# Two of the output's 32 weight heads, loaded in 64 small pieces between the K and V loads

## The chip, the core and the metric

The kernel runs on one core of a Trainium2 chip. Its time is the device time of one execution in microseconds (us). PE is TensorE (matmuls, with their weight loads shown as PEld), ACT is ScalarE, DVE is VectorE, POOL is GpSimd, SP is SyncE, from whose queue nearly all transfers are issued; 16 transfer (DMA) engines carry them out.

## The reference

One step of decoding: attention with a long cache, multiplied by a gate that a small dense block computes. All is float32.

```python
# x: 2 x 1 x 512; 32 query heads, 8 K/V heads, 32768 cached keys, 128 per head; wq 512 x 4096, wo 4096 x 512
xn = layernorm(x)
q = (xn @ wq) as 2 x 32 x 1 x 128
scores = q . k_cache * 128 ** -0.5        # each K/V head serves 4 query heads
o = softmax(scores) . v_cache             # 2 x 32 x 128
s = o as 2 x 4096 @ wo                    # the output's weights: 32 heads of 128 x 512
h = max(xn @ w1 + b1, 0) ** 2             # 512 -> 1792
g = silu(h @ w2 + b2)                     # 1792 -> 512
return x + s * g
```

K and V are 2 x 8 x 32768 x 128 numbers each, 268 MB, and are read once.

## The kernel before

The host lays the inputs out so that each transfer is a plain block. The 16 pairs of a batch entry and a K/V head (`NS`) are the turns of a loop. Each turn takes four blocks of 128 rows by 64 KB, 8192 KB each: K in two halves (transposed, `in_kt`), V in two halves (`in_vt`). They go in turn into two tiles in SBUF, `slot0` and `slot1`; the query weights (`in_wq`) and the dense block's weights (`in_wm`) are the first two blocks that pass through these slots.

PE, ACT and DVE run the turns in a hardware loop; SP and POOL have their instructions written out. In a turn, `scores(0)` and `scores(1)` multiply K's halves with the queries into the PSUM banks `sc`; DVE and PE find the maximum, ACT takes the exponentials, PE transposes them (`tp`, `pT`), and two passes over V's halves add up in `o_ps`; at the end of the turn these are copied, transposed (`ot`) and scaled into a column of `oT`. Behind each pass over a slot PE counts its semaphore up, and `release` issues the next load into that slot, which waits in SP's queue for this count. So while one load runs, the next one is issued as soon as PE is through with the other slot. An instruction in SP's queue that waits holds up those behind it.

The output's weights `wo` have a place of their own in SBUF, `wo_sb`, 32 heads of 512 numbers on each of 128 rows. They are issued from SP directly behind the last V load, in pieces of 16, 8, 5 and 2 heads (`PIECES`) and one more head in two halves, each with a semaphore of its own (`piece0` to `piece5`). After the loop PE multiplies heads 0 to 23 as they come (the matmuls into `wb`, in which each head is one matmul 512 wide), ACT copies their sum, and PE adds it up together with heads 24 to 31 in `sc` (matmuls 64 wide); DVE multiplies by the gate and adds x in one scan, and SP stores the result. The gate comes from the dense block, which runs before the loop.

`AHEAD` is a number of semaphore clears that SP runs between the load of `in_wm` and the first K load; they have no effect on the data.

Of the kernel before, what the change touches and what calls it, by code (L numbers as in the profile page):

```python
# [15 lines left out]
P = 128  # L16
B, D, HQ, HKV, SK, DH, F = 2, 512, 32, 8, 32768, 128, 1792
REP = HQ // HKV
NS = B * HKV
# [6 lines left out]
FJ = FG // 32  # L26
SLOT = HALF
NSLOT = 2
PIECES = (16, 8, 5, 2)
WIDE = 24  # L30
AHEAD = 9
HN = P // 2
SCALE = 1.0 / math.sqrt(DH)

# [88 lines left out]
        return self.sem, self.n  # L123


def build(nc, x22, x8, kt, vt, wq, wm, wo, out):
    pe, act, dve = (Looped(nc, e, n) for e, n in ((nc.tensor, "pe"), (nc.scalar, "act"), (nc.vector, "dve")))
    pool, sp = (Engine(nc, e, n) for e, n in ((nc.gpsimd, "pool"), (nc.sync, "sp")))

    def mm(*args, **kw):  # L130
        pe.do("matmul", *args, **kw)
# [4 lines left out]
    def sb(name, *shape):  # L136
        return nc.alloc_sbuf_tensor(name, [P, *shape], F32)

    slots = [sb(f"slot{i}", SLOT) for i in range(NSLOT)]
    wo_sb = sb("wo_sb", HQ * D)  # L140
# [15 lines left out]

    slot_sem = [nc.alloc_semaphore(f"slot{i}") for i in range(NSLOT)]
    piece_sem = [nc.alloc_semaphore(f"piece{i}") for i in range(len(PIECES) + 2)]
    small_sem, xe_sem, out_sem = (nc.alloc_semaphore(n) for n in ("small", "xe", "out"))
    count = [0] * NSLOT  # L160
    free = [None] * NSLOT
# [2 lines left out]
    def load(src, width):  # L164
        i = issued[0] % NSLOT
        issued[0] += 1
        if free[i] is not None:
            sp.wait(free[i])
        count[i] += 16
        nc.sync.dma_start(slots[i][:, 0:width], src).then_inc(slot_sem[i], 16)  # L170
        return i, (slot_sem[i], count[i])

    stream = [load(wq, SLOT), load(wm, 2 * FJ * D)]
    for _ in range(AHEAD):
        nc.sync.sem_clear(out_sem)
    todo = [(x[s, u], SLOT) for s in range(NS) for x in (kt, vt) for u in range(2)]

    def release(token):
        free[stream.pop(0)[0]] = token
        if todo:  # L180
            stream.append(load(*todo.pop(0)))
            if not todo:
                h = 0
                for n, sem in zip(PIECES, piece_sem):
                    nc.sync.dma_start(wo_sb[:, h * D:(h + n) * D], wo[h * P:(h + n) * P].rearrange("(p h) e -> p (h e)", h=n)).then_inc(sem, 16)
                    h += n
                for u in range(2):
                    nc.sync.dma_start(wo_sb[:, h * D + u * NG * HN:h * D + (u + 1) * NG * HN],
                                      wo[h * P + u * HN:h * P + (u + 1) * HN].rearrange("r (t e) -> (r t) e", t=2)).then_inc(piece_sem[len(PIECES) + u], 16)


    g = nc.gpsimd
    t = pool.done(g.memset(ident[:, :], 0.0))
# [12 lines left out]
    for u in range(2):  # L206
# [5 lines left out]
    t = dve.done("tensor_reduce", selh[:, :], ident[:, :].rearrange("p (a h) -> p h a", h=REP), axis=AX.X, op=ALU.add)  # L212
# [10 lines left out]
    t = pe.done()  # L223
    dve.wait(t)
    t = dve.done("tensor_copy", xs[:, :], ms[:, 0:22])
    pe.wait(t, t_one)
    mm(ms[:, 32:40], mean[:, :], xs[:, 0:8], start=True, stop=True)
    t = pe.done()
    dve.wait(t)
    t = dve.done("tensor_reduce", st[:, 2:4], ms[:, 32:40].rearrange("p (d b) -> p b d", b=B), axis=AX.X, op=ALU.add)  # L230
    dve.wait(t)
    t = dve.done("tensor_tensor", xc[:, :].rearrange("p (d b) -> p d b", b=B), xs[:, 0:8].rearrange("p (d b) -> p d b", b=B),
                                 st[:, None, 2:4].to_broadcast([P, ND, B]), op=ALU.add)
    dve.wait(t)
    t = dve.done("tensor_mul", sq[:, :], xc[:, :], xc[:, :])
    pe.wait(t)
    mm(ms[:, 64:72], mean[:, :], sq[:, :], start=True, stop=True)
    t = pe.done()
    dve.wait(t)
    t = dve.done("tensor_reduce", st[:, 4:6], ms[:, 64:72].rearrange("p (d b) -> p b d", b=B), axis=AX.X, op=ALU.add)  # L240
    dve.wait(t)
    t = dve.done("tensor_scalar", st[:, 6:8], st[:, 4:6], -1.0, 1e-5, op0=ALU.mult, op1=ALU.add)
    act.wait(t)
    t = act.done("activation", st[:, 8:10], st[:, 6:8], AF.Sqrt)
    dve.wait(t)
    t = dve.done("reciprocal", st[:, 10:12], st[:, 8:10])
# [5 lines left out]
    i, t = stream[0]  # L252
    pe.wait(t_x, t, t_selg)
    for d in range(ND):
        for f in range(2):
            for c in range(NG):
                lo = d * HQ * DH + (f * NG + c) * W
                mm(sc[f][32 * c:32 * c + 32, :], xT[:, d, :], slots[i][:, lo:lo + W], start=(d == 0), stop=(d == ND - 1))
    t = pe.done()
# [3 lines left out]
    for f in range(2):  # L263
# [3 lines left out]
        t = pe.done()  # L267
# [70 lines left out]
    for s in range(NS):  # L338
# [4 lines left out]
        t_s, t = scores(1)  # L343
# [3 lines left out]
        t = dve.done("tensor_reduce", r1[:, :], rm[:, :], axis=AX.X, op=ALU.max)  # L347
        pe.wait(t, *([t_rs] if t_rs else []))
        tr(ms[:, :P], r1[:, :].to_broadcast([P, P]), ident[:, :])
        t = pe.done()  # L350
        dve.wait(t)
        t = dve.done("tensor_reduce", mh[:, :], ms[:, :P].rearrange("p (a h) -> p h a", h=REP), axis=AX.X, op=ALU.max)
        dve.wait(t)
        t = dve.done("tensor_mul", mm4[:, :], mh[:, :], seln[:, :])
        dve.wait(t)
        t = dve.done("tensor_reduce", nm[:, :], mm4[:, :], axis=AX.X, op=ALU.add)
# [5 lines left out]
        for u in range(2):  # L362
# [3 lines left out]
            t = pe.done()  # L366
# [4 lines left out]
        t = pe.done()  # L371
        dve.wait(t)
        t_rs = dve.done("reciprocal", rs[:, :], ms[:, :REP])
        for u in range(2):
            i, t = stream[0]
            pe.wait(t, t_pT[u], t_osb)
            for n in range(32):
                y = n % NG
                k, r = divmod(n, 8)
                lo = k * 32 + r * 4  # L380
# [7 lines left out]
        for n in range(4):  # L388
            lo = n * (P - REP)
# [11 lines left out]
    def heads(h, u):  # L401
        hkv, k = divmod(h, REP)
        lo = 2 * hkv * REP * 16 + (1 - u) * REP + k
        return oT[:, lo:lo + 31 * REP + 1:REP]
# [3 lines left out]
    h = 0  # L408
# [6 lines left out]
        for c in range(NG):  # L415
            mm(acc[32 * c:32 * c + 32, 0:2 * HN:2], heads(h, u), wt[:, h, los[c]:los[c] + HN], start=False, stop=stop)

    for n, sem in zip(PIECES, piece_sem):
        if h == WIDE:
            pe.wait(t_w)  # L420
            for u in range(2):
                for c in range(NG):
                    lo = c * P + u * HN
                    mm(acc[32 * c:32 * c + 32, 0:2 * HN:2], selg[:, 32 - u:64 - u], o_sb[:, lo:lo + HN], start=(u == 0), stop=False)
        pe.wait((sem, 16))
        for h in range(h, h + n):
            if h < WIDE:
                c = h % NG
                mm(wb[32 * c:32 * c + 32, :], heads(h, 0), wt[:, h, :], start=(h < NG), stop=(h >= WIDE - NG))
                if h == WIDE - 1:  # L430
                    t = pe.done()
                    act.wait(t, t_otr)
                    t_w = act.done("copy", o_sb[:, :], wb[:, :])
                continue
            pe.wait(t_res)
            if h // REP == HKV - 1:
                pe.wait(t_o)
            for u in range(2):
                narrow(h, u, [c * P + u * HN for c in range(NG)], False)
        h += 1  # L440
    for u in range(2):
        pe.wait((piece_sem[len(PIECES) + u], 16))
        narrow(h, u, [(u * NG + c) * HN for c in range(NG)], u == 1)
    t = pe.done()
    dve.wait(t, t_gate)
    t = dve.done("tensor_tensor_scan", yb[:, :], gate[:, :], acc[:, :2 * HN], 0.0, op0=ALU.mult, op1=ALU.add)
    sp.wait(t)
    nc.sync.dma_start(out, yb[:, :]).then_inc(out_sem, 16)
    used = sorted(x.num for x in [e.sem for e in (pe, act, dve, pool, sp)] + slot_sem + piece_sem + [small_sem, xe_sem])
    nc.sync.sem_clear(range(used[0], used[-1] + 1))  # L450
    nc.sync.wait_ge(out_sem, 16)
    for e in (pe, act, dve):
# [8 lines left out]
def packed(A_x, A_k_cache, A_v_cache, A_wq, A_wo, B_w1, B_b1, B_w2, B_b2):  # L461

    def c(a):
        return np.ascontiguousarray(a)

    x = np.asarray(A_x).reshape(B, D)
    k = np.asarray(A_k_cache).transpose(1, 0, 3, 2).reshape(NS, DH, 2, HALF).transpose(0, 2, 1, 3)
    v = np.asarray(A_v_cache).transpose(1, 0, 2, 3).reshape(NS, 2, NG, NJ, 4, P, DH).transpose(0, 1, 5, 4, 2, 3, 6).reshape(NS, 2, P, SLOT)
    wq = np.asarray(A_wq).reshape(ND, P, HQ * DH).transpose(1, 0, 2).reshape(P, SLOT)
    w1 = np.asarray(B_w1).reshape(ND, P, F).transpose(1, 0, 2).reshape(P, ND * F)  # L470
    w2 = np.asarray(B_w2).reshape(NG, FJ, 32, D).transpose(0, 2, 1, 3).reshape(P, FJ * D)
    w = np.asarray(A_wo).reshape(HQ, DH, D)
    parts, h = [], 0
    for n in PIECES:
        parts.append(w[h:h + n].transpose(1, 0, 2).reshape(n * P, D))
        h += n
    last = w[h].reshape(DH, NG, 2, HN)
    parts += [last[:, :, u].reshape(HN, D) for u in range(2)]
    rows = [x.reshape(B, ND, P).transpose(1, 0, 2).reshape(B * ND, P),
            np.asarray(B_b1).reshape(NG, FJ, 32).transpose(1, 0, 2).reshape(FJ, P)]  # L480
    x4 = x.reshape(B, NG, 2, HN).transpose(2, 1, 0, 3)
    b4 = np.repeat(np.asarray(B_b2).reshape(NG, 2, HN).transpose(1, 0, 2)[:, :, None], B, axis=2)
    eight = [a.reshape(2 * NG * B, HN) for a in (x4, b4)]
    return {"x22": c(np.concatenate(rows)), "x8": c(np.concatenate(eight, axis=1)), "kt": c(k), "vt": c(v), "wq": c(wq),
            "wm": c(np.concatenate([w1, w2], axis=1)), "wo": c(np.concatenate(parts))}


# [13 lines left out]
```

## Time and profile before

| | us |
|---|---|
| median of 3 runs | 1302.91 (1302.81 to 1303.24) |
| the profiled execution | 1302.98 |
| its span, from first to last instruction | 1301.7 |
| busy: PE / PEld / ACT / DVE / POOL | 672.9 / 208.6 / 79.1 / 49.5 / 5.6 |
| K and V loads | 64 of 8192 KB |
| bytes read from HBM | 561.01 MB |
| mean granted clock of PE | 0.734 of full speed |

The profile gives for each engine its busy time, then transfers by queue, then the chain of work that ended last, followed back from the last instruction. Busy times are averages over stages with different limits, so the stages are also read one by one: as windows of time, as the chain in order of time, and as lists of waits, in which "A <- B" means that A stood idle until B was done. For a transfer the time from issue to landing includes the time for which it queued behind others. Nearly all instructions of PE, ACT and DVE carry one line number, that of the helper that puts them into the program (L64), so groups are named by their tiles.

### The profile page before, as it was taken

The numbers are of one execution on the slowest core, as the hardware profiler recorded it, in microseconds if no ns is written. First come the engines' busy times: TensorE is split into PE (matmuls) and PEld (weight loads), VectorE is DVE, ScalarE is ACT, GpSimd is POOL, SyncE is SP. The second block draws the span as 40 slices with busy tenths as digits, with TensorE's granted clock in tenths as the row PEclk, the third lists the DMA queues.
The fourth block names the chain that finished last, engine by engine and source line by source line (L and its number), as shares of the span: only waits on it lengthen the run. The fifth ranks groups of instructions, "written<-read, shape, count | busy, mean of one in ns | idle before, by whom it ended". The sixth has DMA issues, their size and how long they took to land.

```text
span 1301.7 us, 10377 instructions
## 1 busy us (share of the span) xinstructions
PE 672.9 (52%) x4713; PEld 208.6 (16%) x4713; DVE 49.5 (4%) x165; ACT 79.1 (6%) x139; POOL 5.6 (0%) x30
## 2 busy tenths in 40 slices
PE   3445445535536545545645545554654654554565
PEld 1111111211112111111211111121111211111122
DVE  0000000000000000000000000000000000000000
ACT  1010010100001010010101001010010101001010
POOL 0000000000000000000000000000000000000000
PEclk9777677678677778667677767767767767767777
DMA  9999999999999999999999999999999999999998
GB/s 412 428 446 425 443 425 445 419 443 427 429 441 427 443 427 443 423 445 421 443 427 427 443 427 443 427 443 421 445 423 441 429 427 443 427 443 425 445 421 363
DMA packets 10583, 561.17 MB, mean 431 GB/s; under 512 B 1195, under 2 KB 1617, under 8 KB 1745
## 3 DMA queue, kind: packets, MB, share of 16 engines
q1 hardware_dynamic: 10512, 561.06, 99.7%
q8 instruction: 5, 0.08, 0.0%
q10 hardware_dynamic: 65, 0.02, 0.0%
q14 instruction: 1, 0.01, 0.0%
HBM read 561.01 MB, written 0.07 MB: 431 GB/s over the span
## 4 chain that ended last, share of the span: by engine, by line
DMA 75%; PE 24%; issue 1%; DVE 0%; ACT 0%; SPq 0%; ACTq 0%
DMA slot<-in_vt 36%; DMA slot<-in_kt 36%; PE sc L64 12%; PE o_ps L64 11%; DMA slot<-in_wm 3%; PE wb L64 1%; DVE hT L64 0%; ACT o_sb L64 0%; DVE o_sb L64 0%; PE ot L64 0%; DVE yb L64 0%; SPq L170 0%; ACT sc L64 0%; ACTq L454 0%; ACTq L102 0%
## 5 line engine op out<-in xcount | busy, mean ns | idle before, releaser
L64 PE MATMUL sc<-slot,qz 128*32 128x512 f32 x2048 | 295.5, 742 | 299.6 <-DMA slot<-in_kt 299.6
L64 PE MATMUL o_ps<-slot,pT 128*16 128x512 f32 x2048 | 294.4, 739 | 209.0 <-DMA slot<-in_vt 209.0
L64 PEld LDWEIGHTS sc<-slot,qz 128*32 128x32 f32 x2048 | 81.0, 133 | 503.3 <-issue 503.3
L64 PEld LDWEIGHTS o_ps<-slot,pT 128*16 128x16 f32 x2048 | 69.3, 113 | 420.7 <-issue 420.7
L64 ACT ACT_TABLE_LOAD x19 | 24.4, 1283 | 650.3 <-DVE nm L64 647.3
L64 PE MATMUL tp<-ident,prob 128*128 128x128 f32 x136 | 31.2, 403 | 53.2 <-ACT prob L64 53.2
L64 DVE TENSOR_REDUCE rm<-sc 128x1 f32<-128x512 f32 x32 | 22.1, 691 | 574.9 <-PE sc L64 574.9
L64 ACT COPY o_sb<-o_ps 128x512 f32<-128x512 f32 x16 | 9.4, 586 | 504.8 <-PE o_ps L64 504.8
L64 PEld LDWEIGHTS tp<-ident,prob 128*128 128x128 f32 x136 | 24.0, 206 | 57.7 <-issue 55.7
L64 DVE TENSOR_REDUCE t<-ot 128x4 f32<-128x64 f32 x16 | 3.6, 224 | 524.2 <-PE ot L64 524.2
L64 ACT ACTIVATE prob<-sc,nm 128x512 f32<-128x512 f32 x32 | 21.7, 683 | 0.2
L64 ACT COPY pT<-tp 128x512 f32<-128x512 f32 x32 | 18.8, 586 | 13.8 <-PE tp L64 13.8
L64 PE MATMUL sc<-slot,xT 128*32 128x512 f32 x64 | 8.6, 695 | 17.7 <-DMA slot<-in_wq 17.7
L64 PE MATMUL ot<-ident,o_sb 128*128 128x128 f32 x64 | 10.1, 280 | 13.7 <-ACT o_sb L64 12.8
L64 PEld LDWEIGHTS ms<-selh,l 128*128 128x128 f32 x64 | 15.6, 334 | 0.0
L64 PE MATMUL ms<-ident,r 128*128 128x128 f32 x16 | 4.7, 294 | 20.0 <-DVE r L64 20.0
L64 PE MATMUL ms<-selh,l 128*128 128x4 f32 x64 | 13.7, 319 | 0.0
L64 PEld LDWEIGHTS ot<-ident,o_sb 128*128 128x128 f32 x64 | 6.7, 141 | 27.9 <-issue 27.9
L64 PE MATMUL wb<-slot,xT 128*32 128x448 f32 x32 | 4.8, 762 | 6.4 <-DMA slot<-in_wm 6.4
L275 POOL COPY qz<-qT 128x4 f32<-128x4 f32 x16 | 3.0, 187 | 1167.2 <-PE sc L64 1137.2
L64 PEld LDWEIGHTS ms<-ident,r 128*128 128x128 f32 x16 | 2.1, 133 | 34.1 <-issue 34.1
L64 ACT ACTIVATION_READ_ACCUMULATOR prob<-sc,nm 128x1 f32 x32 | 6.3, 196 | 0.0
(63 smaller groups left out, 55.4 us busy)
## 6 DMA issues: line engine op xcount, KB each, us to landing
slot<-in_wm SPq DMA_DIRECT2D x1, 7168.0 KB, 38.4
wo_sb<-in_wo SPq DMA_DIRECT2D x1, 4096.0 KB, 39.1
wo_sb<-in_wo SPq DMA_DIRECT2D x1, 2048.0 KB, 43.5
wo_sb<-in_wo SPq DMA_DIRECT2D x1, 1280.0 KB, 45.8
slot<-in_kt SPq DMA_DIRECT2D x32, 29.1
slot<-in_vt SPq DMA_DIRECT2D x32, 29.1
wo_sb<-in_wo SPq DMA_DIRECT2D x1, 512.0 KB, 46.6
wo_sb<-in_wo SPq DMA_DIRECT2D x2, 128.0 KB, 46.4
```

The costliest lines, as they stand in the source:

```text
L64: instruction = getattr(self.e, name)(*[x(i) if callable(x) else x for x in args], **kw)
L275: return pool.done(g.tensor_copy(qz[:, 28:32], qT[:, b, hkv, :]))
```

## The change

The first piece has 14 heads instead of 16. The two heads that it loses, 0 and 1 (`EARLY`), get an input of their own, `in_we`, cut by the host into 64 blocks of 16 rows of 512 bytes, 8 KB each. Behind each of the 64 K and V loads, `bit` issues one of these blocks from the same queue into its place in `wo_sb`: 32 for head 0 (8 groups of 16 rows, 4 quarters of the width), then 32 for head 1. Each head's 32 blocks count on one semaphore (`early0`, `early1`), and PE waits for each count ahead of that head's first matmul. `AHEAD` goes from nine to one. The last V load, the weights' remaining pieces and PE's matmuls stay in their order.

```diff
-PIECES = (16, 8, 5, 2)
+PIECES = (14, 8, 5, 2)
+EARLY = HQ - 1 - sum(PIECES)
 WIDE = 24
-AHEAD = 9
+AHEAD = 1
...
+    def bit():
+        n = 2 * NS * 2 - len(todo) - 1
+        h, n = divmod(n, 4 * P // 16)
+        g, q = divmod(n, 4)
+        lo = h * D + q * P
+        nc.sync.dma_start(wo_sb[16 * g:16 * g + 16, lo:lo + P], we[h, g, q]).then_inc(early_sem[h], 16)
+
     def release(token):
         free[stream.pop(0)[0]] = token
         if todo:
             stream.append(load(*todo.pop(0)))
+            bit()
             if not todo:
-                h = 0
+                h = EARLY
...
-    for n, sem in zip(PIECES, piece_sem):
+    parts = [(1, (sem, 16 * (4 * P // 16))) for sem in early_sem] + [(n, (sem, 16)) for n, sem in zip(PIECES, piece_sem)]
+    for n, t in parts:
...
-        pe.wait((sem, 16))
+        pe.wait(t)
...
+    early = w[:EARLY].reshape(EARLY, P // 16, 16, 4, P).transpose(0, 1, 3, 2, 4)
+    parts, h = [], EARLY
```

SP's queue at the start, from the loads of the query weights and of the dense block on. An entry gives its line, what it moves, and in brackets the semaphore for which it waits (`pe` is PE's count). Before:

```order
L170 DMA slot<-in_wq 128x16384 [waits barrier_Pool_Activation_PE_DVE_SP_release]
L170 DMA slot<-in_wm 128x14336
L175 ISA x9
L170 DMA slot<-in_kt 128x16384 [waits pe] x2
L170 DMA slot<-in_vt 128x16384 [waits pe] x2
L170 DMA slot<-in_kt 128x16384 [waits pe] x2
```

And now:

```order
L172 DMA slot<-in_wq 128x16384 [waits barrier_Pool_Activation_PE_DVE_SP_release]
L172 DMA slot<-in_wm 128x14336
L177 ISA
L172 DMA slot<-in_kt 128x16384 [waits pe]
L185 DMA wo_sb<-in_we 16x128
L172 DMA slot<-in_kt 128x16384 [waits pe]
L185 DMA wo_sb<-in_we 16x128
L172 DMA slot<-in_vt 128x16384 [waits pe]
```

A small load, which waits for nothing itself, stands between each load and the wait of the next; of the nine clears one is left.

SP's queue at the end, from the last two V loads on. Before:

```order
L170 DMA slot<-in_vt 128x16384 [waits pe] x2
L185 DMA wo_sb<-in_wo 128x8192
L185 DMA wo_sb<-in_wo 128x4096
L185 DMA wo_sb<-in_wo 128x2560
L185 DMA wo_sb<-in_wo 128x1024
L188 DMA wo_sb<-in_wo 128x256 x2
L448 DMA out<-yb 128x128 [waits dve]
```

And now:

```order
L172 DMA slot<-in_vt 128x16384 [waits pe]
L185 DMA wo_sb<-in_we 16x128
L172 DMA slot<-in_vt 128x16384 [waits pe]
L185 DMA wo_sb<-in_we 16x128
L195 DMA wo_sb<-in_wo 128x7168
L195 DMA wo_sb<-in_wo 128x4096
L195 DMA wo_sb<-in_wo 128x2560
L195 DMA wo_sb<-in_wo 128x1024
```

The last small load stands ahead of the first piece, which is two heads narrower (7168 numbers a row instead of 8192); the pieces behind it are the same.

PE behind the loop, where the heads' matmuls begin. Before:

```order
L64 MATMUL wb<-wo_sb,oT 32x512 [waits piece0]
L64 MATMUL wb<-wo_sb,oT 32x512 x15
L64 MATMUL wb<-wo_sb,oT 32x512 [waits piece1]
L64 MATMUL wb<-wo_sb,oT 32x512 x7
L64 MATMUL sc<-o_sb,selg 32x64 [waits act]
```

And now:

```order
L65 MATMUL wb<-wo_sb,oT 32x512 [waits early0]
L65 MATMUL wb<-wo_sb,oT 32x512 [waits early1]
L65 MATMUL wb<-wo_sb,oT 32x512 [waits piece0]
L65 MATMUL wb<-wo_sb,oT 32x512 x13
L65 MATMUL wb<-wo_sb,oT 32x512 [waits piece1]
L65 MATMUL wb<-wo_sb,oT 32x512 x7
```

The same 24 matmuls stand in the same order; the first two wait for the small loads' counts and no longer for the first piece.

More of the change, by code (lines that the diff above doesn't have):

```diff
@@ L123, in done, with build @@
         return self.sem, self.n
-def build(nc, x22, x8, kt, vt, wq, wm, wo, out):
+def build(nc, x22, x8, kt, vt, wq, wm, we, wo, out):
     pe, act, dve = (Looped(nc, e, n) for e, n in ((nc.tensor, "pe"), (nc.scalar, "act"), (nc.vector, "dve")))
@@ L158, in build @@
     piece_sem = [nc.alloc_semaphore(f"piece{i}") for i in range(len(PIECES) + 2)]
+    early_sem = [nc.alloc_semaphore(f"early{i}") for i in range(EARLY)]
     small_sem, xe_sem, out_sem = (nc.alloc_semaphore(n) for n in ("small", "xe", "out"))
@@ L181, in release @@
             stream.append(load(*todo.pop(0)))
+            bit()
             if not todo:
-                h = 0
+                h = EARLY
                 for n, sem in zip(PIECES, piece_sem):
-                    nc.sync.dma_start(wo_sb[:, h * D:(h + n) * D], wo[h * P:(h + n) * P].rearrange("(p h) e -> p (h e)", h=n)).then_inc(sem, 16)
+                    nc.sync.dma_start(wo_sb[:, h * D:(h + n) * D], wo[(h - EARLY) * P:(h - EARLY + n) * P].rearrange("(p h) e -> p (h e)", h=n)).then_inc(sem, 16)
                     h += n
@@ L188, in release @@
                     nc.sync.dma_start(wo_sb[:, h * D + u * NG * HN:h * D + (u + 1) * NG * HN],
-                                      wo[h * P + u * HN:h * P + (u + 1) * HN].rearrange("r (t e) -> (r t) e", t=2)).then_inc(piece_sem[len(PIECES) + u], 16)
+                                      wo[(h - EARLY) * P + u * HN:(h - EARLY) * P + (u + 1) * HN].rearrange("r (t e) -> (r t) e", t=2)).then_inc(piece_sem[len(PIECES) + u], 16)
     g = nc.gpsimd
@@ L448, in build @@
     nc.sync.dma_start(out, yb[:, :]).then_inc(out_sem, 16)
-    used = sorted(x.num for x in [e.sem for e in (pe, act, dve, pool, sp)] + slot_sem + piece_sem + [small_sem, xe_sem])
+    used = sorted(x.num for x in [e.sem for e in (pe, act, dve, pool, sp)] + slot_sem + piece_sem + [small_sem, xe_sem] + early_sem)
     nc.sync.sem_clear(range(used[0], used[-1] + 1))
@@ L472, in packed @@
     w = np.asarray(A_wo).reshape(HQ, DH, D)
-    parts, h = [], 0
+    early = w[:EARLY].reshape(EARLY, P // 16, 16, 4, P).transpose(0, 1, 3, 2, 4)
+    parts, h = [], EARLY
     for n in PIECES:
@@ L484, in packed @@
     return {"x22": c(np.concatenate(rows)), "x8": c(np.concatenate(eight, axis=1)), "kt": c(k), "vt": c(v), "wq": c(wq),
-            "wm": c(np.concatenate([w1, w2], axis=1)), "wo": c(np.concatenate(parts))}
+            "wm": c(np.concatenate([w1, w2], axis=1)), "we": c(early), "wo": c(np.concatenate(parts))}
 def kernel(**inputs):
```

## The prediction

> **What bounds the kernel now.** I read the page first: the busy shares, the transfers, the chain that ended last.
>
> ```profile
> PE 672.9 (52%) x4713; PEld 208.6 (16%) x4713; DVE 49.5 (4%) x165; ACT 79.1 (6%) x139; POOL 5.6 (0%) x30
> DMA  9999999999999999999999999999999999999998
> q1 hardware_dynamic: 10512, 561.06, 99.7%
> DMA 75%; PE 24%; issue 1%; DVE 0%; ACT 0%; SPq 0%; ACTq 0%
> ```
>
> No compute engine is busy for more than half of the span, while the packets of SyncE's queue (q1) fill 99.7% of 16 transfer engines. The chain gives PE 24% all the same, so the next view is the chain in order of time, to see whether PE's share is a real second bound. Columns: start, length, what.
>
> ```profile
> 50.24 29.31 DMA slot<-in_kt
> ...
> 1202.35 9.32 PE o_ps L64 x64
> ...
> 1240.95 8.81 PE sc L64 x64
> 1249.76 0.02 issue
> 1249.78 29.75 DMA slot<-in_vt
> 1279.53 0.22 issue
> 1279.75 9.88 PE o_ps L64 x64
> ...
> 1291.06 5.36 PE wb L64 x48
> 1296.42 0.02 issue
> 1296.45 0.59 ACT o_sb L64
> 1297.04 0.04 issue
> 1297.09 2.52 PE sc L64 x142
> 1299.60 0.02 issue
> 1299.62 0.42 DVE yb L64
> ```
>
> The chain goes from a landing to PE's 9 us on that slot, from there to the issue of the next load into it, and 29 us later that load lands. But only the first part of those 29 us is free: the load issued at 1249.78 stands behind the one issued before it, which is still running. The pace shows it. The load that landed at 50.24 + 29.31 = 79.55 is the second of the 64 K and V loads, the one at 1279.53 is the last, 62 loads further: (1279.53 - 79.55)/62 = 19.354 us for 8192 KB, 433 GB/s. The windows say that nothing is idle there (columns: window, its length, busy of each engine, granted clock, DMA share, GB/s):
>
> ```profile
> 98.86:1240.84 1141.98, 593.46 (x4018) 180.76 (x4018) 39.13 (x129) 63.43 (x113) 2.62 (x14) 0.72 1.00 433
> 1279.75:1285.38 5.63, 5.63 (x28) 1.28 (x32) 0.00 (x0) 0.00 (x0) 0.00 (x0) 0.50 0.99 425
> 1285.38:1289.62 4.24, 4.20 (x40) 0.94 (x32) 0.00 (x0) 0.00 (x0) 0.00 (x0) 1.00 0.95 406
> ```
>
> So up to the last V landing at 1279.53 the time is bytes over a full pipe: share 1.00 for 1142 us. From there PE leads: 9.88 us on V, the copy and transposes, 48 matmuls on `wb` in 5.36, the copy, `sc` in 2.52, the scan, the store. Beside it runs the transfer of the output's weights, 8192 KB (4096 + 2048 + 1280 + 512 + 2 x 128). Whether that ends before PE or after decides what a smaller remainder is worth, so the third reading is the issues and landings of these pieces (KB each, us from issue to landing; then SyncE's issues with their start):
>
> ```profile
> wo_sb<-in_wo SPq DMA_DIRECT2D x1, 4096.0 KB, 39.1
> wo_sb<-in_wo SPq DMA_DIRECT2D x1, 512.0 KB, 46.6
> wo_sb<-in_wo SPq DMA_DIRECT2D x2, 128.0 KB, 46.4
> out<-yb SPq DMA_DIRECT2D x1, 64.0 KB, 1.6
> ```
> ```profile
> 1250.15 2.12 SPq L185 DMA_DIRECT2D wo_sb<-in_wo  x4
> 1251.85 0.42 SPq L185 DMA_DIRECT2D wo_sb<-in_wo  x1
> 1252.32 0.91 SPq L188 DMA_DIRECT2D wo_sb<-in_wo  x2
> ```
>
> The first piece lands at 1250.15 + 39.1 = 1289.25, the 512 KB piece at 1251.85 + 46.6 = 1298.45, the last half at about 1252.80 + 46.4 = 1299.2 (the second issue of the pair starts some 0.48 behind the first). PE's `sc` group ends at 1297.09 + 2.52 = 1299.61, and its last four matmul pairs are the only ones that need that half. Transfers and PE end within a few tenths of each other. PE's waits in the last 22 us say the same:
>
> ```profile
> PE o_ps L64 <- DMA slot<-in_vt: 10.1, 1, 10.1
> PEld wb L64 <- DMA wo_sb<-in_wo: 0.4, 1, 0.4
> ```
>
> The one wait put down to the output's weights is 0.4 us of a weight load, and the matmuls of the group behind it run on without a break (48 in 5.36 us is 0.11 each). Taking bytes away here therefore frees at most about 0.4 us, and likelier nothing.
>
> **The change part by part.**
>
> *512 KB leave the first piece* (16 heads become 14). At 19.354/8192 = 2.363 ns per KB this is 1.21 us of transfer behind the last V landing. PE leads there, so I cost it at zero; bounds 0 to -0.4 us from the row above.
>
> *64 loads of 8 KB join the stream.* Their bytes are the same 1.21 us in sum, 0.0189 us each, but 63 of the 64 now run ahead of the last V landing, in a window whose DMA share is 1.00: no gap takes them up. On top comes what a transfer costs beyond its bytes, which no row shows for 8 KB. The nearest rows are the five pieces that queue behind the first: from 1289.25 to 1299.2, 9.95 us for 4096 KB, where bytes give 9.68, so 0.27 more or 0.055 a piece. Each has 128 rows, 8 for each of 16 engines if they are shared out evenly, and a completion. If the 0.055 is spread over these nine, a small load (16 rows, so one row and one completion for each engine) costs 0.012; if all of it is the completion, 0.055; at the low end nothing. I take 0.012, an even sharing, since no row sets a completion apart from the data rows beside it. So 0.031 us a load (0.019 to 0.074), and the last V lands 63 x 0.031 = 1.95 us later (1.2 to 4.7).
>
> The Trainium skill, page "DMA: Bandwidth & Descriptors", section "Bandwidth", speaks against the change: transfers under 64 KB are dominated by their descriptors, and a 4 KB transfer keeps the transfer engines 0.68 us. By 0.68 each, an estimate from that page, the sum would be 63 x 0.68 = 43 us, against 1.95 by the pieces. That figure is for transfers issued by GpSimd; the two halves here, of 128 rows too, land with the 512 KB piece before them within 0.75 us, 0.60 of it bytes, so this trace disagrees with it for transfers that queue behind others.
>
> *64 issues more on SyncE.* An issue with its own shape is 0.42 us (row at 1251.85). They stand behind the load's issue, and the next thing in SyncE's queue is the wait for PE to give a slot back:
>
> ```profile
> SPq L170 <- PE sc L64: 636.7, 33, 29.2
> SPq L170 <- PE o_ps L64: 570.8, 30, 19.7
> ```
>
> These 63 waits come to 1207.5 us, 19 each, so 0.42 is covered; it would show only if a slot came free within 0.42 us of the issue before. Only the last one delays something, the six issues of the weights, by 0.4 us, and these land 37 us after issue or later. Eight fillers fewer on SyncE (nine to one): they run at the start, where SyncE waits for PE anyway. Zero.
>
> *Two more waits on PE*, for heads 0 and 1. The last small load stands directly behind the last V load and lands some 0.1 us after it, 11 us before PE's `wb` group. Zero, even with that cover halved.
>
> *PE behind the later landing.* PE's work on the last V is not of fixed length. It ran at a granted clock of 0.50 until 1285.38 and at 1.00 from there (windows above). The same 64 matmuls took 9.32, 8.81 and 9.88 us in three quoted places of the chain. If the clock rises at 1285.38 again, a start 1.95 later has 1.95 less at half speed, does 0.975 less work there, and so ends only 0.975 later: 8.90 us. If the rise follows PE's start, it stays 9.88 and the end is 1.95 later. I take the middle, 9.39, which is also about the mean of the three (9.34): end 1.46 later. Behind it all is as before.
>
> *Transfers' end.* 64 x 0.031 - 1.21 = 0.77 us later, 1300.0, while PE comes to that half 1.46 later than before: no wait.
>
> **Sum.** 0 + 1.46 us on the profiled execution's 1302.98 (span 1301.7) is 1304.44. That execution lies 0.07 above the median of the runs, 1302.91, so I forecast **1304.4 us**, 0.1% slower. About 0.2%, 2.6 us, is what a measurement of this kernel can tell from no change, so that counts as the same. Ends of the sum: with 0.019 a load, the clock's rise fixed and 0.4 won, 1.19 x 0.5 - 0.4 = +0.2, 1303.1; with 0.074 a load and the clock following, +4.7, 1307.6.
>
> **The rivals.**
>
> *Fixed costs decide (slower).* The small load's completion waits for the writes ahead of it and holds the row of the next load, 63 times. For it: a full pipe has no room, and 0.055 a piece is compatible with it. With the clock following, (2.6/63 =) 0.041 us a load is the point from which the loss exceeds the measurement's bound; at the upper end, 0.074, it gives 1307.6. If each held the engines for the whole latency, at most the 1.6 us in which the 64 KB store lands, it would be 101 us, 1404; against that stand the two halves, both down within 0.75 us. The Trainium skill, page "DMA: Bandwidth & Descriptors", section "Queues, rings and completion order", has a rule that points this way: a completion count is a strongly ordered write, which lands only behind every earlier write of that engine. No row here shows how long the engine itself is held by one.
>
> *The stream takes them up (no loss or a small gain).* The slices of the last 12.4 us (0.31 us each) show that the 16 engines don't end together:
>
> ```profile
> DMA  8989897899997999889999973222220000003300
> ```
>
> From 0.9 the share falls to 0.3 and then 0.2 at about 1296.8 and stays there till 1298.7: a quarter of the engines is nearly 2 us behind the rest. The others have that much slack at each landing. But all 16 get a row of each small load, so the late quarter pays too. If it paid nothing, V would land as before and the tail would win at most 0.4: 1302.5 to 1302.9.
>
> *The tail is bound by transfers after all (a gain).* Then 1.21 us fewer behind V would show in full while the stream loses less; but the total of bytes is unchanged and each engine's work only grows, so even this ends at -0.4, 1302.5. A gain above 0.2% needs a stream faster than its 1.00 share; no row has that.
>
> *A code fetch moves.* SyncE's program grows by 56 instructions. Around 1255, when SyncE had issued the weights, one instruction fetch ran among the loads (its queue: packets, MB, share of 16 engines over 2 us):
>
> ```profile
> q14 instruction: 1, 0.01, 1.0%
> ```
>
> That is 0.3 us of one engine. If it is SyncE's, it now comes in mid-stream, or twice; where it hits an engine of the late quarter, V lands another 0.3 to 0.6 us later: 1304.9.
>
> **How the numbers follow.** Forecast's own mechanism 0.67 (its own range 1303.1 to 1305.5), code fetch besides 0.05, taken up by the stream 0.08, tail bound by transfers 0.04, fixed costs 0.16, of which 0.03 are far above 1307.6. Below 1300.3 lies only a stream that runs faster, 0.03 in all, taken from the two cases of gain. Slower by over 0.2% (from 1305.5): the 0.16 of fixed costs and 0.01 of the fetch. Same: 0.80. Range: from 1302.8, which takes in half of the stream's case, to 1307.6, the bound of the unknown cost.
>
> **What would show it.** The pace of the K and V landings should go from 19.354 to about 19.385, the last V should land near 1281.5, PE's work on it should be under 9.9 us, the first piece should be 3584 KB and land some 1.2 us nearer to the last V than now. SyncE's waits for PE should shrink by 0.4 each and nothing else on its queue. I am wrong if the pace rises above 19.43, which means a cost beyond the bound of 0.074, or if it stays at 19.354, which means that the pipe was not full.

## The result, and the profile after

The changed kernel takes 1309.76 us (median of 6 runs, 1308.39 to 1310.99), the one before 1302.88 (1302.80 to 1303.24): ratio 1.0052, 95% interval 1.0039 to 1.0065. The forecast was 1304.4, no change within 0.2%, in a range that ended at 1307.6. The loss is 6.9 us.

The profiled execution of the change took 1310.99, the slowest of the six, and has a span of 1309.7 us, 8.0 more than before; what is read from it below therefore accounts for 8.0 us and not for 6.9 (the 1.1 between them are some 0.02 us a load, an estimate from 62 loads). Its page, the lines that answer to those shown ahead of the prediction:

```profile
PE 672.1 (51%) x4713; PEld 208.0 (16%) x4713; DVE 49.5 (4%) x165; ACT 79.1 (6%) x139; POOL 5.6 (0%) x30
DMA  9999999999999999999999999999999999999998
q1 hardware_dynamic: 12560, 561.06, 99.7%
DMA 75%; PE 24%; issue 1%; DVE 0%; ACT 0%; SPq 0%; ACTq 0%
```

By these lines hardly anything has happened: the same engines' work, the same bytes, the same full pipe, 2048 more packets (64 x 32, so 16 rows and 16 completions for each small load). A share of 99.7% says only that packets were under way, not how fast they went. The chain in order of time says where the loss is:

```profile
52.20 27.45 DMA slot<-in_kt
...
1259.47 28.94 DMA slot<-in_vt
1288.41 0.22 issue
1288.63 9.09 PE o_ps L65 x64
...
1299.15 5.36 PE wb L65 x48
1304.52 0.02 issue
1304.54 0.59 ACT o_sb L65
1305.13 0.04 issue
1305.18 2.45 PE sc L65 x138
1307.62 0.02 issue
1307.65 0.42 DVE yb L65
```

The second K load lands at 52.20 + 27.45 = 79.65 (79.55 before), the last V at 1288.41 (1279.53 before). The pace over 62 loads is (1288.41 - 79.65)/62 = 19.496 us a load, 0.142 above the 19.354 of before, where the forecast had 0.031. All of the loss, and more, is made there: V is 8.88 later, the span's end 8.0, because PE gives 0.79 back on the last V (9.09 us for 9.88). The windows agree (columns as before):

```profile
98.86:1240.84 1141.98, 590.91 (x4018) 179.79 (x4018) 39.16 (x129) 63.43 (x113) 2.63 (x14) 0.73 1.00 431
1288.63:1297.72 9.09, 9.05 (x64) 2.11 (x64) 0.00 (x0) 0.00 (x0) 0.00 (x0) 0.78 0.98 421
```

In the same stretch of 1142 us the share is 1.00 as before, and the rate is 431 GB/s instead of 433, although the small loads' bytes count in it.

### The profile page after: what moved, and what is told of

It is laid out like the page before. It is cut to its first block, busy times and chain, and to the rows that moved or that the text cites. A ratio compares the mean times of both kernels' runs of the same rounds, so it can differ in the third digit from the quotient of the medians.

```text
span 1309.7 us, 10433 instructions
## 1 busy us (share of the span) xinstructions
PE 672.1 (51%) x4713; PEld 208.0 (16%) x4713; DVE 49.5 (4%) x165; ACT 79.1 (6%) x139; POOL 5.6 (0%) x30
## 3 DMA queue, kind: packets, MB, share of 16 engines
q1 hardware_dynamic: 12560, 561.06, 99.7%
## 4 chain that ended last, share of the span: by engine, by line
DMA 75%; PE 24%; issue 1%; DVE 0%; ACT 0%; SPq 0%; ACTq 0%
DMA slot<-in_vt 36%; DMA slot<-in_kt 36%; PE sc L65 12%; PE o_ps L65 11%; DMA slot<-in_wm 3%; PE wb L65 1%; DVE hT L65 0%; ACT o_sb L65 0%; DVE o_sb L65 0%; PE ot L65 0%; DVE yb L65 0%; SPq L172 0%; ACT sc L65 0%; ACTq L465 0%; ACTq L103 0%
## 5 line engine op out<-in xcount | busy, mean ns | idle before, releaser
L65 PE MATMUL wb<-slot,hT 128*32 128x512 f32 x28 | 5.3, 846 | 2.1 <-DVE hT L65 2.1
## 6 DMA issues: line engine op xcount, KB each, us to landing
wo_sb<-in_wo SPq DMA_DIRECT2D x1, 3584.0 KB, 36.6
```

The source lines that it names most:

```text
L65: instruction = getattr(self.e, name)(*[x(i) if callable(x) else x for x in args], **kw)
```

## The experiments

Of the 0.142 us that a K or V load has become slower, 0.019 are the small load's bytes at the stream's pace. What makes the other 0.123? The runs were chosen to tell apart a cost of the second completion, of the short row, and of the place in SBUF to which the rows go. In all of them I read the pace as above, from the landing of the second K load to that of the last V (in the first run, of the last K). Of each edit the lines that decide are shown; "..." marks what is left out, the host's layout of `in_we` and the counts for which PE waits among it.

Three theories were on record before these runs. Completion: the small load's completion, close behind the large one's, holds the engines. Row: a short row among long ones costs time. Place: rows that go to partitions into which other engines are writing hold those engines up.

**One more completion, no small load.** Each load through the slots is cut into two halves of the width.

```diff
-        count[i] += 16
-        nc.sync.dma_start(slots[i][:, 0:width], src).then_inc(slot_sem[i], 16)
+        for lo in (0, width // 2):
+            count[i] += 16
+            nc.sync.dma_start(slots[i][:, lo:lo + width // 2], src[:, lo:lo + width // 2]).then_inc(slot_sem[i], 16)
...
```

> The kernel before, with each of the 66 loads through the slots cut into two loads of half the width (128 rows of 32 KB), each with its own completion; no small loads. Three theories for the 0.14 us that each K and V load has become slower (19.354 to 19.496 us), of which 0.03 are bytes and descriptors. Completion theory: a second completion close behind a load's own holds the engines until the first is through; here the two completions lie 9.7 us apart, so only 0.04 us of descriptors are added and the pace is 19.40. Row theory: a short row (512 bytes) breaks the run of long ones; no short rows here, so 19.40 as well. Place theory: the 16 rows go to partitions that other engines serve; none here, 19.40. A rival in which any further completion costs 0.1 us gives 19.46 to 19.50, and a time near 1309.

Measured: 1307.69 (one run, 1302.91 for the kernel before on the same chip). In its chain the second K load and the last K load, 60 loads further, land at 79.84 and 1245.42:

```profile
50.43 29.41 DMA slot<-in_kt
...
1215.82 29.60 DMA slot<-in_kt
```

The pace is 19.426, 0.072 above before: 0.008 for each of the nine further descriptors that an engine has (a descriptor is one entry that an engine carries out, here 8 rows and a completion). All three theories had 19.40, 0.04 above before; a rival in which any further completion costs 0.1 had 19.46 to 19.50. The result lies between, nearer to 19.40, so a second completion 9.7 us away from the first doesn't cost the 0.12 that is looked for.

**Fewer and longer rows: 16 heads early, 64 loads of 16 rows of 4 KB.**

```diff
-PIECES = (14, 8, 5, 2)
+PIECES = (8, 5, 2)
...
+        j, g = divmod(n, 8)
+        lo = 2 * j * D
+        nc.sync.dma_start(wo_sb[16 * g:16 * g + 16, lo:lo + 2 * D], we[j, g]).then_inc(early_sem[j], 16)
...
```

> Sixteen heads early: 64 loads of 16 rows of 4 KB (64 KB each), one behind each K and V load, so 4096 KB more in the stream: 0.151 us of bytes a load. A load's own completion and the small one's are now about 0.16 us apart instead of 0.03. Completion theory: most of the hold is covered by the longer row, pace 19.354 + 0.151 + 0.012 = 19.52 to 19.55. Row theory (a shorter row than 64 KB costs 0.11 whatever its length): 19.63. Place theory (cost grows with the bytes that go to other engines' partitions, here eight times as many): 19.63 and up to 20.4.

Measured: 1348.65 (one run). Its chain:

```profile
51.97 28.89 DMA slot<-in_kt
...
1294.63 31.71 DMA slot<-in_vt
```

From 80.86 to 1326.34 the pace is 20.09: 0.734 more than before, of which 0.151 are the 64 KB. So 0.58 are left where the change has 0.12. With the completions further apart the cost is nearly five times as high, where the completion theory had 19.55 at most; the row theory, 0.11 for any row shorter than 64 KB, gave 19.63. Neither fits. Of the three, only that of the place allowed this much.

**The same bytes in 128 rows of 512 bytes.** Sixteen heads again, 64 KB in each small load, but a row for every partition.

```diff
...
+        h, q = divmod(n, 4)
         lo = h * D + q * P
...
+        nc.sync.dma_start(wo_sb[:, lo:lo + P], we[h, q]).then_inc(early_sem[h], 16)
...
```

> Sixteen heads early: 64 loads of 128 rows of 512 bytes (64 KB each), one behind each K and V load; each engine has 8 short rows of the partitions that it also serves in the large loads. The two completions are 0.19 us apart. Completion theory: 19.354 + 0.151 + 0.044 for nine descriptors = 19.55. Row theory: eight short rows of 0.11 each, 20.4, or 19.66 if only the first counts. Place theory: no row leaves its engine's partitions, 19.55.

Measured: 1317.58 (one run), from 80.07 to 1294.26 a pace of 19.584:

```profile
52.47 27.60 DMA slot<-in_kt
...
1264.20 30.06 DMA slot<-in_vt
```

0.230 above before, less 0.151 of bytes: 0.079 for nine descriptors, about as in the run with split loads. There are eight times as many short rows as in the change, and less is paid beyond the bytes than its 0.123. A short row by itself is not the cost.

**The change's two heads in 8 loads of 128 rows**, one behind every eighth K or V load.

```diff
+        if n % 8 != 0:
+            return
+        h, q = divmod(n // 8, 4)
         lo = h * D + q * P
...
+        nc.sync.dma_start(wo_sb[:, lo:lo + P], we[h, q]).then_inc(early_sem[h], 16)
...
```

> The changed kernel with its two early heads in 8 loads of 128 rows of 512 bytes (64 KB), one behind every eighth K and V load, instead of 64 loads of 16 rows. The same bytes and the same number of short rows for each engine, an eighth of the completions. Completion theory: the last V lands 8 x (0.151 + 0.044) = 1.6 us later than before, and about 1 to 1.6 us of this reach the end: 1303.9 to 1304.5. Row theory: the loss of the changed kernel stays, 1309. Place theory: as completion theory.

Measured: 1304.29 (10 runs, 1303.67 to 1305.04), ratio to before 1.0010, interval 1.000 to 1.002. The last V lands at 1281.29, 1.76 later than before, where 1.6 was expected:

```profile
1251.68 29.61 DMA slot<-in_vt
```

With rows on all partitions the costs that the forecast took from the pieces come out. But this run also has only an eighth of the completions, so by itself it doesn't part the place from them; the next run does.

**The change with its 16 rows 8 partitions apart.** Number, size and order of the loads and their completions stay; only the place of the rows differs.

```diff
-        nc.sync.dma_start(wo_sb[16 * g:16 * g + 16, lo:lo + P], we[h, g, q]).then_inc(early_sem[h], 16)
+        nc.sync.dma_start(wo_sb[g:P:8, lo:lo + P], we[h, g, q]).then_inc(early_sem[h], 16)
...
```

> The changed kernel, but the 16 rows of each small load lie 8 partitions apart over all 128 instead of side by side. Sizes, counts and order are as in the changed kernel. Place theory (rows written into partitions that other engines are writing at full rate hold those engines up): if each engine serves 8 partitions side by side in the large loads, every small row is now its own engine's, and the pace falls from 19.496 to 19.354 + 0.019 + 0.016 = 19.39, the time to 1304 to 1306. If the engines' partitions are interleaved, half as many rows meet at one place and about half of the 0.107 us stays: 19.44, 1306 to 1307.5. Row theory and completion theory: nothing changes, 19.50 and 1308 to 1311.

Measured: 1305.17 (10 runs, 1304.38 to 1305.87), ratio 1.0017, interval 1.0007 to 1.0026, against 1309.76 for the change. Its last loads and what follows:

```profile
52.81 26.90 DMA slot<-in_kt
...
1253.84 28.71 DMA slot<-in_vt
1282.55 0.22 issue
1282.77 9.28 PE o_ps L65 x64
```

The pace is (1282.55 - 79.71)/62 = 19.401. Beyond its bytes a small load now costs 0.027, not 0.123. Nothing but the rows' place was changed, so 0.10 of the 0.142 is the place, and the completion and row theories, which had 19.50 here, fall. The 16 rows of 4 KB were then set 8 apart too:

```diff
-        nc.sync.dma_start(wo_sb[16 * g:16 * g + 16, lo:lo + 2 * D], we[j, g]).then_inc(early_sem[j], 16)
+        nc.sync.dma_start(wo_sb[g:P:8, lo:lo + 2 * D], we[j, g]).then_inc(early_sem[j], 16)
...
```

> Sixteen heads early by 64 loads of 16 rows of 4 KB as before (pace about 20.05, time 1348.65), with the 16 rows 8 partitions apart. Place theory: 19.354 + 0.151 + 0.016 = 19.52 if each engine serves 8 partitions side by side, about 19.8 if they are interleaved. A theory in which one long row by itself costs 0.5: 20.05 and 1348 again.

Measured: 1337.31 (one run) for 1348.65 side by side:

```profile
49.91 30.59 DMA slot<-in_kt
...
1283.43 31.12 DMA slot<-in_vt
```

V lands at 1314.55, and from 80.50 on the pace is 19.904. That is 0.40 beyond the bytes, down from 0.58 only, so 8 apart is not yet free. Neither of the two forms of the place theory holds in both runs. With 8 KB the first came out, in which each engine serves 8 partitions side by side (19.401 for 19.39, where the second had 19.44). With 64 KB it fails (19.52), and the second, in which about half of the cost stays, is nearer (19.904 for 19.8). Why 0.027 of 0.123 stays in the one and 0.40 of 0.58 in the other is not shown.

**Is it crowding, or any foreign place?** A foreign place is one into which another engine writes in the large loads; crowding means that many rows meet at few places. The Trainium skill, page "SBUF — State Buffer", section "Door 1: The DMA port swizzle", says that the partitions share 16 ports, four neighbours and the four 32 further on to a port, and that a transfer's bandwidth depends on how many of these ports its partitions reach. By that map 16 rows side by side fill 4 ports, 16 rows 8 apart fill 8, and rows 4 apart over all 128 fill all 16. Two runs with one size and one number, 64 loads of 32 rows of 2 KB, differ in the rows' place alone ("-" is the first run, "+" the second):

```diff
-        nc.sync.dma_start(wo_sb[g:P:4, lo:lo + D], we[j, g]).then_inc(early_sem[j], 16)
+        nc.sync.dma_start(wo_sb[32 * g:32 * g + 32, lo:lo + D], we[j, g]).then_inc(early_sem[j], 16)
...
```

> Sixteen heads early by 64 loads of 32 rows of 2 KB (64 KB), the rows 4 partitions apart over all 128. Crowding theory: the partitions share 16 doors, four neighbours and the four 32 further on to a door, and a small load costs what its fullest door needs beyond its own bytes; side by side 16 rows fill 4 doors (pace 20.05 with 4 KB rows), 8 apart they fill 8 (19.87), here all 16 doors get 4 KB each, so little is left: 19.354 + 0.151 + 0.03 = 19.53, at most 19.68. Foreign-place theory: it is enough that a row lies where another engine writes, crowded or not; then at least as many bytes are foreign as 8 apart and the pace stays near 19.87. Row theory: 2 KB rows lie between 512 bytes (0.03) and 4 KB (0.35 to 0.5), some 19.7.

> The same 64 loads of 32 rows of 2 KB, with the 32 rows side by side: the one difference to the run before is where the rows lie. Crowding theory: 8 doors get 8 KB each, as with 16 rows of 4 KB that lie 8 apart, so the pace is about that one's, 19.85, and the time near 1337. Row theory and foreign-place theory: the same pace as with the rows 4 apart.

Measured: 1313.82 with the rows 4 apart, 1343.22 side by side (one run each). Their chains, first 4 apart:

```profile
52.29 27.41 DMA slot<-in_kt
...
1260.49 29.89 DMA slot<-in_vt
```

and side by side:

```profile
53.11 27.62 DMA slot<-in_kt
...
1289.33 30.83 DMA slot<-in_vt
```

The paces are 19.527 and 19.991: 0.022 and 0.485 beyond the bytes. Row, number, size, completions and source are the same; 29 us lie between them through the place alone. 19.53 was expected for the one by crowding; by the foreign-place theory both had some 19.87, by the row theory 19.7, and these two fall. For the other run crowding had 19.85, taken as about the pace of the 16 rows 8 apart. That pace was 19.904, so 0.087 more is not explained. With 64 KB a load, the cost beyond the bytes is 0.58 for 16 rows side by side, 0.49 for 32 side by side, 0.40 for 16 rows 8 apart, 0.08 for 128 rows and 0.02 for 32 rows 4 apart. By the map of the Trainium skill (the same page and section) these five fill 4, 8, 8, 16 and 16 ports, so the traces agree with it in order. No run here watches a port itself.

The records of single packets in the traces show which work becomes slower. Between 98.86 and 1240.84 us a 64 KB row of a K or V load takes 2422 ns in the median in the change, 2420 before. But 15 of the 128 rows of a load take over 2450 ns, where before it is 0.2, and the mean goes from 2421.7 to 2435.9. Each engine has 8 of these rows in a load, so this is 0.11 us, most of the 0.123. The rows that run beside a small row average 2477, the others 2423. With the small rows 8 apart the mean is 2423.7. With 32 rows side by side it is 2476.6, with 32 rows 4 apart 2422.2; eight times the difference is 0.44 of the 0.46 us between their paces. So the small load does not hold the whole stream: it lengthens a few of the large rows beside it.

**SyncE's clears, and the change again.** Nine clears with the change, and, later and on another chip, the change again:

```diff
-AHEAD = 1
+AHEAD = 9
```

> The changed kernel with nine clears on SyncE as before instead of one. If the place of SyncE's instructions (a code fetch in mid-stream) is a part of the loss, the time moves by more than 1 us from 1309.8; by the place theory it doesn't: 1308 to 1311, pace 19.50.

> The changed kernel once more, on this chip beside the others, as the measure for the run with nine clears (1311.39) and for the one with rows 8 apart (1305.17). If the clears count for nothing, its time overlaps 1311.2 to 1311.6 or lies within the scatter that it had, 1308.4 to 1311.

Measured: 1311.39 with nine (4 runs, 1311.21 to 1311.58), 1310.46 for the change again (4 runs, 1309.89 to 1312.19); from 79.50 to 1288.93 and from 79.90 to 1289.31 both paces are 19.507. With nine clears the time was outside the expected 1308 to 1311 and 1.6 above 1309.76, which by the expectation would have made the clears a part of the loss. The change again took up to 1312.19, though, so 1311.39 lies within its own scatter. And the move is upward: to put the eight clears back wins nothing.

**Both heads in one load behind the first K load.**

```diff
+        if 2 * NS * 2 - len(todo) - 1 == 0:
+            nc.sync.dma_start(wo_sb[:, 0:EARLY * D], we).then_inc(early_sem[0], 16)
```

> The changed kernel with its two early heads in a single load of 128 rows of 4 KB behind the first K load: the bytes still go ahead of the V loads, with one further completion in all. By the forecast's own terms the last V lands 1.21 + 0.02 us later than before and 0.6 to 1.2 us of that reach the end: 1303.5 to 1304.1. If 512 KB less behind the last V are worth something by themselves, it is below 1303.

Measured: 1303.60 (10 runs, 1303.26 to 1304.07), ratio 1.0005, interval 0.9996 to 1.0015: as expected, not told apart from before, and no sign of a gain. The last V lands 1.16 later, at 1280.69, and PE takes 8.87 us on it, 1.01 less than before:

```profile
1251.62 29.06 DMA slot<-in_vt
1280.69 0.22 issue
1280.90 8.87 PE o_ps L65 x64
```

No run here beat the kernel before; in every one that brings heads ahead of the last V, that V lands later, by about their bytes (1.16 for 1.21 us here) or by more.

## Why the prediction was wrong

*What bounds the kernel* was read rightly: a full pipe up to the last V, PE from there. All of the loss lies in the pace, and the run with one load gives no sign that 512 KB less behind V win anything by themselves. Of the 0.4 us of waiting for the output's weights, which I took as the most that could be won, 0.3 stand in the waits of the change too:

```profile
PEld wb L65 <- DMA wo_sb<-in_wo: 0.3, 1, 0.3
```

*The step that failed* is the small load's cost beyond its bytes: 0.012 us taken, 0.055 as the upper bound, 0.123 measured. Both came from the five pieces behind the first, and 0.012 was taken "since no row sets a completion apart from the data rows beside it". But the question was not rows or completion. Every piece has 128 rows, one for each partition; the small load has 16 that lie side by side. I set "16 rows, so one row and one completion for each engine" and looked at the engines' side of the transfer alone, never at the side where the rows arrive. What it left out is the lengthening of the K and V rows beside the small load: 0.10 us goes when the same rows are set 8 apart, and 0.027 is left. For loads that reach all partitions the row was nearer: nine descriptors, 0.055 by it, cost 0.072 in the split run and 0.079 with 128 rows. The range was too narrow by the same step: 63 x 0.074 = 4.7 was its end, 8.9 came, and the pace went past the 19.43 that the prediction gave as its sign of being wrong.

*The rival "fixed costs decide"* had the right sign, a cost once a load, at 0.16, but by luck: its mechanism was the completion, and the run with rows 8 apart has the same completions and costs 0.027. Its upper end of 0.074 was too low too. The Trainium skill, page "DMA: Bandwidth & Descriptors", section "Bandwidth", has 0.68 us for a transfer of 4 KB, by which, as an estimate, the sum would be 43 us; measured are 0.142 a load, so for transfers that queue behind others the trace still disagrees with it.

*The clock.* PE's work on the last V took 9.09 us, after 9.88; 9.39 was forecast from half the gain. It ran 4.05 us at a granted clock of 0.50 and from 1292.68 at 1.00; before it was 5.63 us, up to 1285.38. So the rise came 7.30 later for a start 8.88 later, and neither form of the prediction holds (a rise fixed in time, or one that follows PE's start). The same group on a V half takes 8.54, 8.66 and 9.09 us in the last three turns of the change, so that the sum came near 9.39 is in part luck; less than 1 us hangs on it. One of the three places from which the prediction took its mean (8.81) is the group on a K half, not the same matmuls.

*SyncE.* A small load's issue takes 0.43 us, and the waits for PE shrank from 1207.5 to 1186.5, 0.33 for each of 63, about what was forecast (0.4):

```profile
L185 SPq DMA_DIRECT2D wo_sb<-in_we x64: 417/431/446, 32.1 to 1259.8; - x64
SPq L172 <- PE sc L65: 627.2, 33, 30.0
SPq L172 <- PE o_ps L65: 559.3, 30, 19.3
```

*The code fetch* that ran at 1255 before has moved to mid-stream, as that rival had it (window 737 to 739 us):

```profile
q14 instruction: 1, 0.01, 1.0%
```

Its share is the same. The run with rows 8 apart has a fetch in mid-stream too, between 733 and 741 us, and is 4.6 us faster, so the loss is not in it.

*The first piece* is 3584 KB and lands 36.6 us after its issue at 1260.32, which is 8.5 behind the last V where it was 9.7: 1.2 nearer, as forecast, and 2.2 us before PE's `wb` group begins.

## What to carry to other kernels

Moving a transfer into a stream that is already full delays that stream by about its bytes or more, however small its pieces are; it can only pay where something waits for it later, and here PE hardly did (0.4 us). If small loads must run beside a full stream, spread their rows over all partitions: 32 rows of 2 KB cost 0.02 us beyond their bytes when 4 partitions apart and 0.49 side by side. And a bound taken from a row must come from a transfer of the same shape on both sides; a busy share of 1.00 says nothing about what a new pattern does to the rate.

## What the runs showed of the hardware that was not expected

Transfers whose rows lie side by side in SBUF lengthen rows of other transfers that run beside them: with 64 KB a small load, 16 rows of 4 KB side by side add 0.58 us to each 8192 KB load beyond their own bytes, 32 rows of 2 KB 0.49, while 128 rows of 512 bytes add 0.08 and 32 rows 4 apart 0.02. At 8 KB the place makes 0.123 or 0.027. About 15 of the 128 rows of a K or V load carry the 0.123. Whether these are the rows that go to the crowded partitions stays open, since a packet's record here names neither its engine nor its partition.

A descriptor more for each engine (a row or a completion) costs about 0.008 us in this stream: 0.072 for nine in the split run, 0.079 for nine with 128 rows of 512 bytes, one run each. The packets' own times agree: a row of 512 bytes takes 27 ns, of which 19 are its bytes at the rate of a 64 KB row (2420 ns), and a completion takes 9.
